# Moving the v products to the front, transposing a block of x by DMA, and four smaller re-orderings in a fused attention + MLP kernel

## Chip, cores and metric

One Trainium2 chip, one of its cores. The metric is device time in microseconds (us) of one execution; smaller is better. Each kernel was run several times. A profile is one of those executions, and its span is about 2 us shorter than the time of the same run, so spans are compared with spans and times with times.

Engines are called as the profile calls them: PE (TensorE, matmuls), DVE (VectorE), ACT (ScalarE), POOL (GpSimd), SP (SyncE, which here only issues DMAs; "SPq" in the listings).

## What the kernel must compute

```python
# x: 1 x 2048 x 1024, bf16; all weights bf16
xn  = layernorm(x)
qkv = xn @ wqkv                         # 1024 x 3072; 32 heads of 32
# each token attends to 8 tokens of its past, 2 apart:
logits = einsum(q, k[token - 2*w], w = 0..7) * 32**-0.5   # masked before token 0
s = (softmax(logits) @ v[token - 2*w]) @ wo
g = silu( (silu(xn @ w1) * (xn @ w3)) @ w2 )              # 1024 -> 3584 -> 1024
out = x + s * g
```

Of the kernel before, what the change touches and what calls it, by code (L numbers as in the profile page):

```python
# [8 lines left out]
FP32 = mybir.dt.float32  # L9
BF16 = mybir.dt.bfloat16  # L10
FP16 = mybir.dt.float16
ACTF = mybir.ActivationFunctionType
# [5 lines left out]
def kernel(  # L18
# [12 lines left out]
    P = 128  # L31
# [102 lines left out]
    def k4(name, shape=(2, CH), dt=FP32):  # L134
        return kk.tile([P, *shape], dt, tag="k4", name=name)
# [21 lines left out]
    def act_copy(out_, in_):  # L157
        with hp():
            nc.scalar.copy(out=out_, in_=in_)  # L159
# [3 lines left out]
    def flush():  # L163
        while pend:
            pend.pop(0)()
# [15 lines left out]
    def seven(key, A, B, e11, e12, e22, e21, snap=None):  # L181
        a11, a12, a22, s1, s2, s3, s4 = A
        b11, b21, b22, t1, t2, t3, t4 = B
        if snap is None:
            pa = bank2(f"a{key}")
            for i in I:
                mm(pa[:, i], a11[i], b11, True)
        pe = bank2(f"e{key}")
        for i in I:
            mm(pe[:, i], s1[i], t1, True)  # L190
        pb = bank2(f"b{key}")
        act_copy(pb[:], pa[:] if snap is None else snap)
        sp5 = k4(f"p{key}")
        act_copy(sp5[:], pe[:])
        if snap is None:
            for i in I:
                mm(pa[:, i], a12[i], b21, False)
            e11(pa)
        flush()
        for i in I:  # L200
            mm(pb[:, i], s2[i], t2, False)
        su2 = k4(f"u{key}")
        act_copy(su2[:], pb[:])
        for i in I:
            mm(pe[:, i], s4[i], b22, False)
        e12(pe, su2)
        run_hooks()
        for i in I:
            mm(pb[:, i], s3[i], t3, False)
        e22(pb, sp5)  # L210
        bg(pace["n"])

        def tail():
            for i in I:
                mm(pb[:, i], a22[i], t4, False)
            e21(pb)

        pend.append(tail)
# [74 lines left out]
    def xn_sums(b11, b21, b12, b22, o):  # L293
        nc.vector.tensor_sub(o[:, 0], b12, b11)
        nc.vector.tensor_sub(o[:, 1], b22, o[:, 0])
        nc.vector.tensor_sub(o[:, 2], b22, b12)
        nc.vector.tensor_sub(o[:, 3], b21, o[:, 1])
# [9 lines left out]



    def qkv_sums(w0, w1_, st):  # L310
        lo = lambda w: w.rearrange("p k (c two j) -> p k c two j", two=2, j=4)[:, :, :, 0]
        hi = lambda w: w.rearrange("p k (c two j) -> p k c two j", two=2, j=4)[:, :, :, 1]
        a11, a21, a12, a22 = lo(w0), hi(w0), lo(w1_), hi(w1_)
        s1, s2, s4 = [s.rearrange("p k (c j) -> p k c j", j=4) for s in st]
        s3 = hi(w0.bitcast(FP16))
        nc.vector.tensor_add(s1, a21, a22)
        nc.vector.tensor_sub(s2, s1, a11)
        nc.vector.tensor_sub(s4, a12, s2)
        nc.vector.tensor_sub(s3, a11, a21)
        pace["owed"] += 4.5  # L320

    def qkv_A(w0, w1_, st, g):
# [5 lines left out]
        sp = lambda q: [[sv[q][:, k, 2 * g + i, :] for k in range(KH)] for i in I]  # L328
        return pick(v0, 0), pick(v1, 0), pick(v1, 1), sp(0), sp(1), pick(v3, 1), sp(2)

    def park(t, c, j0, name):
        tl = k4(name, (2, CH), BF16)
        dst = (q_dram, k_dram, v_dram)[t][c, :, j0:j0 + 2, :]

        def fin():
            nc.sync.dma_start(out=dst, in_=tl[:])

        return tl[:], fin

    def qkv_dst(t, c, j0):  # L340
        if c == 0:
# [33 lines left out]
    def att_tile(shape, dt, name):  # L375
        return att.tile([P, *shape], dt, tag="a8", name=name)
# [26 lines left out]
    def scores(c, ws):  # L403
        q = qt[c]
        if c not in sc:
            sc[c] = att_tile((W, CH), BF16, f"Es{c}"), att_tile((NJ, CH), BF16, f"pt{c}")
        E, p_t = sc[c]
        for w in ws:
            o = HALO - DIL * w
            nc.vector.tensor_mul(p_t[:], q[:], kT[:, :, o:o + CH])  # L410
            yield 2.3
            nc.vector.tensor_add(p_t[:, 0:4, :], p_t[:, 0:4, :], p_t[:, 4:8, :])  # L412
            yield 1.25
            nc.vector.tensor_add(p_t[:, 0:2, :], p_t[:, 0:2, :], p_t[:, 2:4, :])
            yield 0.7
            nc.vector.tensor_add(E[:, w, :], p_t[:, 0, :], p_t[:, 1, :])
            yield 0.45
# [139 lines left out]

    tiles = {}

    free = [0, 1, 2, 3, 4, 6, 7, 8, 9]  # L560
    half = [0, 1]
    held = {}

# [57 lines left out]
    def mlp_up(b):  # L621
        work = [(g, fb) for fb in range(HB) for g in I] if b == 0 else []
        work += [(b, fb) for fb in range(HB, FB)]
        order = [fb for fb in range(b * HB, FB)]
        ahead = 2 + b
        for fb in order[:ahead]:
# [237 lines left out]
    def wo(b):  # L864
        (a11, a12, a21, a22, s1, s2, s3, s4), (b11, b12, b21, b22, t1, t2, t3, t4) = wx[b]
        if b == 1:
            xt4 = att_tile((2, 2, 2, CH), BF16, "xw")
            for u in I:
                for dh in I:
                    xw[u, dh] = xt4[:, u, dh]  # L870
                    nc.sync.dma_start(out=xw[u, dh], in_=out_rows(x_flat, 1, u, dh, 1))

        def product(ps, gp, lhs, rhs, first):
            for i in I:
# [43 lines left out]
    def out_rows(ap, b, u, dh, gp):  # L918
        g0 = ((2 * b + u) * NST + gp * 2) * P
        return ap[g0:g0 + 2 * P, dh * CH:(dh + 1) * CH].rearrange("(i p) n -> p i n", p=P)  # L920
# [48 lines left out]
    wq1 = qkv_load(0, 1, slot(6, (4, D)))  # L969
    for st in range(NST):  # L970
        (ln_act if st == 2 else ln_dve)(0, [st])
    qt[0] = att_tile((NJ, CH), BF16, "qt0")
    tps = [ln_tp(0, st, [], busy=(5, 0, 1, 1)[st]) for st in range(NST)]
    for a in I:
# [5 lines left out]
    wk1 = qkv_load(1, 1, rows(0, 4).rearrange("p (k n) -> p k n", k=4))  # L980
    sk = rows(4, 6, FP16).rearrange("p (q k n) -> p q k n", q=3, k=4)
    sk = [sk[:, q] for q in range(3)]
    b12 = k4("b12", (KH, CH), BF16)
    x_load(2)
    ln_dve(1, [0, 1])
    ln_dve(1, [2, 3])

    sq = rows(20, 6, FP16).rearrange("p (q k n) -> p q k n", q=3, k=4)
    sq = [sq[:, q] for q in range(3)]
# [1 line left out]
    Bq = B0, B_of(xT1[0], xT1[1], xT1[3], xs1)  # L991
    def tp1(*sts):
        for st in sts:
            ln_tp(1, st, [(b12[:].unsqueeze(1), slice(0, 1)), (xT[:, 2:3], slice(1, 2))])

    for t, (w0, w1_, ws) in enumerate(((wq0, wq1, sq), (wk0, wk1, sk))):
        first_two(f"f{t}", [qkv_A(w0, w1_, ws, g) for g in range(2)], B0[0], B0[1],
                  snap[2 * t:2 * t + 2], [qkv_copy(t, 0, 2 * g) for g in range(2)],
                  *((lambda: None, 4) if t == 0 else (lambda: tp1(2, 3), 0)))
        if t == 0:  # L1000
            tp1(0, 1)
    qkv_sums(wq0, wq1, sq)
    xn_sums(xT[:, 0], xT[:, 1], b12[:], xT[:, 2], xs)
    qkv_sums(wk0, wk1, sk)
    qkv_seven(0, 0, wq0, wq1, sq, None, snap[0:2])
    x_load(3)
# [4 lines left out]

    tr(2)

    wv = [slot(2 + 4 * h, (4, D)) for h in I]
    sva = slot(0, (2, 4, CH), FP16)
    sv = [sva[:, 0], sva[:, 1], rows(10, 2, FP16).rearrange("p (k n) -> p k n", k=4)]

    def before_v(g):
        if g == 0:
            for h in I:  # L1020
                qkv_load(2, h, wv[h])
            tr(3)
        else:
            with behind("v"):
                qkv_sums(*wv, sv)

# [5 lines left out]
                xn_sums(xT1[0], xT1[1], xT1[2], xT1[3], xs1)  # L1032
        w2_step()
    pace["n"] = PACE[0]
    qkv_seven(2, 0, *wv, sv, step0)
    pace["n"] = PACE[1]
    qkv_seven(1, 1, wk0, wk1, sk, step)
    flush()
    wq0 = qkv_load(0, 0, slot(8, (4, D)))
    wq1 = qkv_load(0, 1, rows(0, 4).rearrange("p (k n) -> p k n", k=4))  # L1040
    qkv_sums(wq0, wq1, sk)
    qkv_seven(2, 1, *wv, sv, step)
    qkv_seven(0, 1, wq0, wq1, sk, step)
    flush()
# [46 lines left out]
```

## The kernel before

Every large product is done block-wise with seven products in place of eight (sums of blocks are formed by DVE first, results recombined by DVE and ACT). Tokens come in four chunks of 512; `qkv_seven(t, b)`, built on `seven`, makes q (t = 0), k (1) or v (2) of the chunk pair b. Its first two products, a11·b11 and a12·b21, need neither sums nor the second chunk of the pair (called the second x block below), so `first_two` can do them early; it keeps a11·b11 as a snapshot for the later steps. The kernel before does that for q and k:

```python
for t, (w0, w1_, ws) in enumerate(((wq0, wq1, sq), (wk0, wk1, sk))):
    first_two(f"f{t}", [qkv_A(w0, w1_, ws, g) for g in range(2)], B0[0], B0[1],
              snap[2*t:2*t+2], ...)          # second x block: transposed by PE in between
    if t == 0:
        tp1(0, 1)
qkv_sums(wq0, wq1, sq)                       # DVE: sums of q's weight blocks
xn_sums(...)                                 # DVE: sums of x's blocks
qkv_seven(0, 0, ...); qkv_seven(1, 0, ...)   # q, k of pair 0
                                             # (v's weights load during the k products, into q's slots)
qkv_seven(2, 0, *wv, ...)                    # v of pair 0
qkv_seven(1, 1, ...)                         # k of pair 1
wq0, wq1 = qkv_load(...), qkv_load(...)      # q's weights once more (2 MB), and their sums
qkv_seven(2, 1, ...); qkv_seven(0, 1, ...)   # v, q of pair 1: the last projections before the MLP
```

Outputs that are not needed at once are parked: copied to a small ring of staging buffers (`k4`) and stored to DRAM by SP.

```python
def park(t, c, j0, name):
    tl = k4(name, (2, CH), BF16)             # the ring also serves the recombination copies
    ...
        nc.sync.dma_start(out=dst, in_=tl[:])
```

The same SP queue also carries the loads of x and of the weights and the DMA transposes of chunks 2 and 3, in order. `seven` releases held-back products (`flush`) early in its order:

```python
    flush()
    for i in I: mm(pb[:, i], s2[i], t2, False)
    su2 = k4(f"u{key}"); act_copy(su2[:], pb[:])
    for i in I: mm(pe[:, i], s4[i], b22, False)
```

Late in the kernel, four pieces of the residual x (`xw`, 256 KB each) load ahead of the `wo` weights.

## Time and profile before

| kernel before | |
|---|---|
| time, median (first 3 runs) | 732.58 us (732.14 to 734.04) |
| time in the later jobs (33 shared runs on three chips) | 731.8 to 735.7 us |
| span of the profiled run | 730.3 us, granted clock 0.998 |
| PE busy | 714.2 us (98%) |

Timeline (start, us, engine, line, operation, output<-inputs, and in brackets the idle time before it and what ended it):

```profile
148.98 1.23 DVE L351 TENSOR_TENSOR pk<-eq,uq 128x1024 bf16<-128x1024 f32 x1 [4.10 <-DMA q_dram<-pk]
167.04 0.69 DVE L603 TENSOR_TENSOR wring<-wring 128x1024 f16<-128x1024 bf16 x1 [1.95 <-DMA t_dram<-wring]
```

ACT's, for the exponential:

```profile
175.46 1.06 ACT L440 ACTIVATE Es<-Es 128x1024 f32<-128x1024 f32 x1 [2.53 <-DVE Es L438]
```

DVE waits for a parked q output to be stored, and 25 us later the exponential waits for DVE. The second line is a link between the two: DVE stands 1.95 us for a store by POOL of sums of w2 (t_dram, landed at 166.94 us), shortly before the operations that lead to the exponential. PE is not named in these lines.

### The profile page before, as it was taken

To read this page: it belongs to the slowest core of one execution; us is meant where nothing else is said; L and a number is where in the kernel's file an instruction comes from. 1 tells how busy PE (TensorE), PEld (TensorE's weight loads), DVE (VectorE), ACT (ScalarE), POOL (GpSimd) and SP (SyncE) were. 2 spreads that over 40 slices of the span, in tenths; PEclk is the share of its full clock that TensorE was granted. 3 is DMA by queue.
4 is the path that set the end of the run, shared out by engine and by line. 5 is a ranking of instruction groups with operands and counts; after the bars stand their busy time and mean duration, and the time that the engine had idled before them with its cause. 6 is when DMAs were issued, how large, how long until landed. Compare 5 with 4: busy or idle time off the path is not lost.

```text
span 730.3 us, 8739 instructions
## 1 busy us (share of the span) xinstructions
PE 714.2 (98%) x3312; PEld 345.8 (47%) x3367; DVE 624.2 (85%) x677; ACT 314.5 (43%) x328; POOL 99.3 (14%) x159
## 2 busy tenths in 40 slices
PE   7999999999999999999999999999999999999996
PEld 4655665654444444444444444444444444444442
DVE  7994688878798879878989899969859999979984
ACT  5744343437554546654545411123454555120233
POOL 0000000010400110142202010010345000510011
PEclk9999999999999999999999999999999999999999
DMA  9379148877756452467755745549799453666505
GB/s 321 140 177 286 57 147 281 254 210 262 200 204 231 143 175 87 141 194 242 231 174 191 240 156 186 178 162 375 188 283 326 136 159 102 192 190 203 179 5 111
DMA packets 117610, 140.82 MB, mean 193 GB/s; under 512 B 14273, under 2 KB 91073, under 8 KB 116929
## 3 DMA queue, kind: packets, MB, share of 16 engines
q1 hardware_dynamic: 103984, 101.47, 44.9%
q0 software_dynamic: 13584, 38.81, 17.2%
q8 instruction: 26, 0.43, 0.3%
q14 instruction: 16, 0.12, 0.1%
HBM read 98.30 MB, written 38.80 MB: 188 GB/s over the span
## 4 chain that ended last, share of the span: by engine, by line
PE 71%; DVE 18%; DMA 4%; issue 3%; ACT 3%; SPq 1%; POOL 0%; DVEq 0%; ACTq 0%; POOLq 0%
PE bm L149 17%; PE am L149 11%; PE em L149 11%; PE db L149 7%; PE bq L149 5%; PE de L149 4%; DVE pt L410 4%; PE eq L149 4%; PE da L149 3%; PE aq L149 3%; PE wb L149 2%; DVE pt L412 2%; PE we L149 2%; PE wa L149 2%; DMA q_dram<-pk 1%
## 5 line engine op out<-in xcount | busy, mean ns | idle before, releaser
L149 PEld LDWEIGHTS <-wring 128*128 128x128 f16 (+1 forms) x1920 | 201.7, 105 | 216.4 <-issue 5.2
L149 PEld LDWEIGHTS <-h_sb 128*128 128x128 f16 (+1 forms) x1088 | 114.0, 105 | 121.7 <-issue 1.0
L149 PE MATMUL bm<-xs,wring 128*128 128x512 f16 x504 | 117.3, 379 | 0.5 <-DVE h_sb L661 0.3
L149 PE MATMUL am<-xT,wring 128*128 128x512 bf16 x322 | 78.8, 379 | 0.9
L410 DVE TENSOR_TENSOR pt<-qt,kT 128x4096 bf16<-128x4096 bf16 x32 | 73.2, 2288 | 0.7
L149 PE MATMUL db<-wring,h_sb 128*128 128x512 f16 x336 | 73.2, 379 | 0.0
L465 DVE TENSOR_TENSOR BC<-Ep,vT 128x2048 bf16<-128x2048 bf16 x56 | 67.0, 1218 | 0.2
L646 DVE TENSOR_TENSOR um<-em,um 128x1024 f32<-128x1024 f32 x28 | 34.2, 1222 | 19.9 <-PE em L149 12.9
L648 ACT ACTIVATE g<-um 128x1024 bf16<-128x1024 f32 x28 | 29.6, 1057 | 49.7 <-DVE um L646 49.7
L149 PE MATMUL da<-wring,h_sb 128*128 128x512 bf16 x219 | 48.9, 379 | 0.3
L451 POOL DMA_DIRECT2D Ep<-pb x64 | 37.9, 600 | 25.5 <-DVE pb L447 18.5
L149 PE MATMUL bm<-h_sb,wring 128*128 128x512 f16 x168 | 39.7, 379 | 0.0
L149 PE MATMUL em<-xs,wring 128*128 128x512 f16 x168 | 39.7, 379 | 0.0
L412 DVE TENSOR_TENSOR pt<-pt 128x2048 bf16<-128x2048 bf16 x32 | 39.1, 1221 | 0.5
L475 DVE TENSOR_TENSOR oT<-oT,BC 128x2048 bf16<-128x2048 bf16 x32 | 39.1, 1220 | 0.5
L149 PE MATMUL em<-xT,wring 128*128 128x512 bf16 x161 | 39.2, 379 | 0.3
L159 ACT COPY bm<-am 128x1024 f32<-128x1024 f32 x28 | 28.0, 999 | 26.1 <-PE am L149 26.1
L159 ACT COPY pm<-em 128x1024 f32<-128x1024 f32 x28 | 28.4, 1013 | 19.3 <-PE em L149 19.2
L159 ACT COPY um<-bm 128x1024 f32<-128x1024 f32 x28 | 28.4, 1013 | 18.6 <-PE bm L149 18.2
L667 ACT CAST g<-bm 128x1024 bf16<-128x1024 f32 x28 | 28.3, 1010 | 17.6 <-PE bm L149 17.6
L351 DVE TENSOR_TENSOR pk<-eq,uq 128x1024 bf16<-128x1024 f32 x12 | 14.7, 1222 | 23.7 <-PE eq L149 13.2
L661 DVE TENSOR_TENSOR h_sb<-bm,pm 128x1024 bf16<-128x1024 f32 x21 | 25.6, 1218 | 5.3 <-PE bm L149 5.3
(176 smaller groups left out, 965.3 us busy)
## 6 DMA issues: line engine op xcount, KB each, us to landing
wring<-in_B_w_dram SPq DMA_DIRECT2D x61, 512.0 KB, 4.4
wring<-t_dram SPq DMA_DIRECT2D x16, 512.0 KB, 5.1
t_dram<-wring POOLq DMA_DIRECT2D x14, 512.0 KB, 4.5
wring<-in_A_wqkv_dram SPq DMA_DIRECT2D x6, 1024.0 KB, 8.0
wring<-t_dram SPq DMA_DIRECT2D x16, 384.0 KB, 5.5
wring<-in_B_w_dram SPq DMA_DIRECT2D x12, 384.0 KB, 4.7
wring<-in_A_x_dram SPq DMA_DIRECT2D x16, 256.0 KB, 6.1
Ep<-pb POOLq DMA_DIRECT2D x64, 64.0 KB, 4.9
```

Source lines behind the costliest of these rows:

```text
L149: anchor["pe"] = nc.tensor.matmul(ps, lhsT=lhs[k], rhs=rhs[k], start=(first and k == 0), stop=(k == n - 1), skip_group_check=not first,)
L159: nc.scalar.copy(out=out_, in_=in_)
L351: anchor["v"] = nc.vector.tensor_add(d, ps[:], a[0][:])
L410: nc.vector.tensor_mul(p_t[:], q[:], kT[:, :, o:o + CH])
L412: nc.vector.tensor_add(p_t[:, 0:4, :], p_t[:, 0:4, :], p_t[:, 4:8, :])
L451: nc.gpsimd.dma_start(out=pr[c][r:P:NR, :, sq * P:(sq + 1) * P], in_=pb[sq * 32:(sq + 1) * 32, :, :])
L465: nc.vector.tensor_mul(dst, E[:, w, :].unsqueeze(1).to_broadcast([P, n, CH]), vT[:, js, o:o + CH])
L475: nc.vector.tensor_add(A, A, B if w0 else C)
L646: v = nc.vector.tensor_add(su2[:], pe[:], su2[:])
L648: nc.scalar.activation(out=hl["g"][:, :, CH:], in_=su2[:], func=ACTF.Silu)
L661: anchor["v"] = nc.vector.tensor_add(h[:, :, CH:], pb[:], sp5[:])
L667: nc.scalar.copy(out=hl["g"][:, :, 0:CH], in_=pb[:])
```

## The change

The intent: do v's first products early as well, so that they cover the time in which DVE forms the sums of the second x block; take the transposes of that block from PE and give them to the DMA; keep v's weights resident so that q's need not be loaded twice; and move some stores, staging buffers, loads and one table load out of the way. The diff, cut to its core (cuts marked "# ..."):

```diff
@@ seven()
             e11(pa)
-        flush()
+            flush()
         for i in I:
             mm(pb[:, i], s2[i], t2, False)
         su2 = k4(f"u{key}")
         act_copy(su2[:], pb[:])
+        flush()                                   # held products one step later (groups with a snapshot)
@@ qkv_sums(..., again=False)
+        if again:                                 # q's sums the second time: 3 in place of 4
+            nc.vector.tensor_sub(s2, a22, s3)
+            nc.vector.tensor_add(s1, s2, a11)
+            nc.vector.tensor_sub(s4, a12, s2)
+            return
@@ park()
+    spare = [0, 1, 10, 11, 2, 3, 10, 11]
-        tl = k4(name, (2, CH), BF16)
+        tl = k4(name, (2, CH), BF16)[:] if t or c < 2 else rows(spare.pop(0), 1)...   # last q outputs
-            nc.sync.dma_start(out=dst, in_=tl[:])
+            (nc.gpsimd if c == 1 else nc.sync).dma_start(out=dst, in_=tl)
@@ mlp_up(b)
+        if b == 0:
+            nc.scalar.activation(out=scr[:], in_=rows(2, 1)[:, 0:1], func=ACTF.Silu)  # early table
@@ mlp_down(): late residual loads
-                    nc.sync.dma_start(out=xw[u, dh], ...)
+                    with behind("dl"):            # behind the wo weights
+                        nc.sync.dma_start(out=xw[u, dh], ...)
@@ start
+    wve = [att_tile((4, D), BF16, f"wve{h}") for h in I]
+    qkv_load(2, 0, wve[0][:])
+    for st in range(NST):
+        ln_dve(1, [st])
+        for a, d in ((0, b12), (1, xT[:, 2])):    # second x block, two half-size transposes a step
+            nc.sync.dma_start(out=d[...], in_=xt[1][...], transpose=True)
+        if st == 1:
+            qkv_load(2, 1, wve[1][:])
-    for t, (w0, w1_, ws) in enumerate(((wq0, wq1, sq), (wk0, wk1, sk))):
+    for t, (w0, w1_, ws) in enumerate(((wq0, wq1, sq), (wk0, wk1, sk), (wve[0][:], wve[1][:], sk))):
         first_two(...)
-        if t == 0:
-            tp1(0, 1)                             # PE transposes
-    wq0 = qkv_load(0, 0, slot(8, (4, D)))         # second load of q's weights
-    wq1 = qkv_load(0, 1, rows(0, 4)...)
-    qkv_sums(wq0, wq1, sk)
+    qkv_sums(wq0, wq1, sk, True)
 # ... (buffer places, the order of free slots, and anchors left out)
```

More of the change, by code (lines that the diff above doesn't have):

```diff
@@ L305, with qkv_sums @@
     B0 = B_of(xT[:, 0], xT[:, 1], xT[:, 2], xs)
-    def qkv_sums(w0, w1_, st):
+    def qkv_sums(w0, w1_, st, again=False):
         lo = lambda w: w.rearrange("p k (c two j) -> p k c two j", two=2, j=4)[:, :, :, 0]
@@ L315, in qkv_sums @@
         s3 = hi(w0.bitcast(FP16))
+        if again:
+            nc.vector.tensor_sub(s2, a22, s3)
+            nc.vector.tensor_add(s1, s2, a11)
+            nc.vector.tensor_sub(s4, a12, s2)
+            pace["owed"] += 3.4
+            return
         nc.vector.tensor_add(s1, a21, a22)
@@ L329, in qkv_A @@
         return pick(v0, 0), pick(v1, 0), pick(v1, 1), sp(0), sp(1), pick(v3, 1), sp(2)
+    spare = [0, 1, 10, 11, 2, 3, 10, 11]
     def park(t, c, j0, name):
-        tl = k4(name, (2, CH), BF16)
+        tl = k4(name, (2, CH), BF16)[:] if t or c < 2 else rows(spare.pop(0), 1).rearrange("p (j n) -> p j n", j=2)
         dst = (q_dram, k_dram, v_dram)[t][c, :, j0:j0 + 2, :]
         def fin():
-            nc.sync.dma_start(out=dst, in_=tl[:])
-        return tl[:], fin
+            (nc.gpsimd if c == 1 else nc.sync).dma_start(out=dst, in_=tl)
+        return tl, fin
     def qkv_dst(t, c, j0):
@@ L405, in scores @@
         if c not in sc:
-            sc[c] = att_tile((W, CH), BF16, f"Es{c}"), att_tile((NJ, CH), BF16, f"pt{c}")
+            sc[c] = att_tile((W, CH), BF16, f"Es{c}"), oT[:, 0] if c == 0 else att_tile((NJ, CH), BF16, f"pt{c}")
         E, p_t = sc[c]
@@ L558 @@
     tiles = {}
-    free = [0, 1, 2, 3, 4, 6, 7, 8, 9]
+    free = [8, 9, 0, 1, 4, 2, 3, 6, 7]
     half = [0, 1]
@@ L870, in wo @@
                     xw[u, dh] = xt4[:, u, dh]
-                    nc.sync.dma_start(out=xw[u, dh], in_=out_rows(x_flat, 1, u, dh, 1))
+                    with behind("dl"):
+                        nc.sync.dma_start(out=xw[u, dh], in_=out_rows(x_flat, 1, u, dh, 1))
         def product(ps, gp, lhs, rhs, first):
@@ L971 @@
         (ln_act if st == 2 else ln_dve)(0, [st])
+    wve = [att_tile((4, D), BF16, f"wve{h}") for h in I]
+    vsn = att_tile((2, 2, CH), FP32, "vsn")
     qt[0] = att_tile((NJ, CH), BF16, "qt0")
@@ L982 @@
     sk = [sk[:, q] for q in range(3)]
-    b12 = k4("b12", (KH, CH), BF16)
+    b12 = rows(12, 2).rearrange("p (k n) -> p k n", k=KH)
+    TPE = ()
+    qkv_load(2, 0, wve[0][:])
+    for st in range(NST):
+        ln_dve(1, [st])
+        if st not in TPE:
+            for a, d in ((0, b12), (1, xT[:, 2])):
+                nc.sync.dma_start(
+                    out=d[:, :, st * P:(st + 1) * P], in_=xt[1][:, st, a * CH:(a + 1) * CH], transpose=True,
+                )
+        if st == 1:
+            qkv_load(2, 1, wve[1][:])
     x_load(2)
-    ln_dve(1, [0, 1])
-    ln_dve(1, [2, 3])
     sq = rows(20, 6, FP16).rearrange("p (q k n) -> p q k n", q=3, k=4)
@@ L993, in tp1 @@
         for st in sts:
-            ln_tp(1, st, [(b12[:].unsqueeze(1), slice(0, 1)), (xT[:, 2:3], slice(1, 2))])
-    for t, (w0, w1_, ws) in enumerate(((wq0, wq1, sq), (wk0, wk1, sk))):
+            ln_tp(1, st, [(b12.unsqueeze(1), slice(0, 1)), (xT[:, 2:3], slice(1, 2))])
+    snap += [vsn[:, 0], vsn[:, 1]]
+    for t, (w0, w1_, ws) in enumerate(((wq0, wq1, sq), (wk0, wk1, sk), (wve[0][:], wve[1][:], sk))):
         first_two(f"f{t}", [qkv_A(w0, w1_, ws, g) for g in range(2)], B0[0], B0[1],
                   snap[2 * t:2 * t + 2], [qkv_copy(t, 0, 2 * g) for g in range(2)],
-                  *((lambda: None, 4) if t == 0 else (lambda: tp1(2, 3), 0)))
-        if t == 0:
-            tp1(0, 1)
+                  *((lambda: None, 4) if t == 0 else (lambda: None, 0)))
+    tp1(*TPE)
     qkv_sums(wq0, wq1, sq)
-    xn_sums(xT[:, 0], xT[:, 1], b12[:], xT[:, 2], xs)
+    xn_sums(xT[:, 0], xT[:, 1], b12, xT[:, 2], xs)
     qkv_sums(wk0, wk1, sk)
@@ L1012 @@
     tr(2)
-    wv = [slot(2 + 4 * h, (4, D)) for h in I]
+    wv = [wve[h][:] for h in I]
     sva = slot(0, (2, 4, CH), FP16)
@@ L1019, in before_v @@
         if g == 0:
-            for h in I:
-                qkv_load(2, h, wv[h])
             tr(3)
-        else:
             with behind("v"):
@@ L1034 @@
     pace["n"] = PACE[0]
-    qkv_seven(2, 0, *wv, sv, step0)
+    qkv_seven(2, 0, *wv, sv, step0, snap[4:6])
     pace["n"] = PACE[1]
@@ L1038 @@
     flush()
-    wq0 = qkv_load(0, 0, slot(8, (4, D)))
-    wq1 = qkv_load(0, 1, rows(0, 4).rearrange("p (k n) -> p k n", k=4))
-    qkv_sums(wq0, wq1, sk)
+    with behind("v"):
+        qkv_sums(wq0, wq1, sk, True)
     qkv_seven(2, 1, *wv, sv, step)
```

## The prediction

> **What bounds the kernel now.** I read the page's busy table first, then what TensorE (PE) waited for, then its timeline where the change works, and last the engines that those waits name.
>
> ```profile
> PE 714.2 (98%) x3312; PEld 345.8 (47%) x3367; DVE 624.2 (85%) x677; ACT 314.5 (43%) x328; POOL 99.3 (14%) x159
> ```
>
> PE is busy 714.2 of 730.3 us. Busy alone does not prove that the array streams, so I checked the pace: eight 128x512 matmuls follow each other in 1.73 us (107 pieces of the chain have just this length), 0.216 us each, from one end of the kernel to the other, and the granted clock is 1.00 until the tail. The kernel is bound by the number of matmuls; the other engines matter only where they make PE wait. Those waits are few:
>
> ```profile
> PE tp L280 <- DVE wring L254: 2.3, 1, 2.3
> PE warm L141 <- DVE warm L138: 1.3, 1, 1.3
> PE am L149 <- ACT bm L159: 0.7, 1, 0.7
> PE eq L149 <- DVE xs L294: 0.5, 1, 0.5
> PE zp L425 <- DVE dsu L823: 0.5, 1, 0.5
> PE bq L149 <- DVE pk L351: 0.3, 1, 0.3
> PE bm L149 <- DVE h_sb L661: 0.3, 1, 0.3
> ```
>
> The columns are total us, times, longest. The first two are the start (first load and layernorm), which the change leaves alone; the tail after the last matmul (about 724.3 to 730.3, output adds and stores) stays too. So 16.1 us of idle PE hold about 4 us of start and 6 us of tail, and everything the change can win back lies in small waits between 13 and 180 us, plus whatever PE work it deletes. That work is here, in PE's timeline (start, us, what, count):
>
> ```profile
> 13.25 7.07 PE L149 MATMUL af<-xT,wring 128*128 128x512 bf16 x32
> 20.15 1.06 PE L280 MATMUL tp<-ident,wring 128*128 128x128 bf16 x16
> 21.04 3.62 PE L149 MATMUL af<-xT,wring 128*128 128x512 bf16 x15
> 24.50 1.06 PE L280 MATMUL tp<-ident,wring 128*128 128x128 bf16 x16
> 25.40 3.62 PE L149 MATMUL af<-xT,h_sb 128*128 128x512 bf16 x16
> 29.57 2.35 PE L149 MATMUL eq<-xs,h_sb 128*128 128x512 f16 x10 [0.54 <-DVE xs L294]
> ```
>
> The two "tp" rows are the transposes of the second x block by matmul; what follows each starts 0.89 and 0.90 us after it. The last row is PE waiting for the first sum of that block.
>
> **What the Trainium skill says.** "DMA: Bandwidth & Descriptors", section "DMA Transpose (X-bar)", allows a transpose during a DMA for 2-byte types from the hardware queue only, with SBUF as the target: the new transposes meet that. The kernel before already has eight of them (128x1024 each), median 3.5 us from issue to landing, 1.3 to 3.3 us of SP's time each, so the trace agrees and prices them. The same page, section "Issuing engines are not separate DMA queues", says a second issuing engine only saves sequencer time, as all share 16 DMA engines; moving the parking stores to POOL should then relieve SP's order, not bandwidth. "SBUF — State Buffer", section "Who interferes with whom", warns that DMAs issued from GpSimd can be starved of descriptors by some VectorE modes; POOL's stores of before to s_dram, t_dram and h_dram land in 3.0 to 4.7 us (medians), SP's parking stores in 2.9 to 5.0, so this trace shows no such starvation. "ScalarE: Activation LUTs", section "What ACT_TABLE_LOAD costs", gives 1283 ns for the load; the trace has 1.28 us.
>
> **The change part by part.**
>
> Transposes: 32 matmuls of 128x128 leave PE, which issues 6672 rows instead of 6736 (weight loads counted). By the starts above that is 0.89 + 0.90 = 1.8 us of the bounding engine, the one certain gain. ACT loses eight PSUM copies of 0.6 us (4.8 us), gains two snapshot copies of 1.0 us. In their place SP issues eight half-size transposes.
>
> Early v products: the same 32 matmuls (32 x 0.216 = 6.9 us) move ahead of the q products, none is added. By PE's order they now stand where DVE's sums of block two were late. DVE reached that first sum at 28.29 us; its queue ahead of it changes by about one 1.2 us sum more and one 0.65 us statistic less. PE will need it at 13.25 + 3 x 6.9 = 33.95 us instead of about 28.9. The 0.7 us wait (0.92 us between starts less one matmul) goes.
>
> The v weights: before, they could only load into slots of q, behind parking stores and transposes on SP:
>
> ```profile
> 54.13 0.34 SPq L336 DMA_DIRECT2D k_dram<-pk  x1
> 54.52 3.32 SPq L291 DMA_TRANSPOSE h_sb<-wring  x1
> 57.93 0.77 SPq L336 DMA_DIRECT2D k_dram<-pk  x1
> 58.75 5.74 SPq L291 DMA_TRANSPOSE h_sb<-wring  x3
> ```
>
> ```profile
> 62.13 1.23 DVE L351 TENSOR_TENSOR pk<-eq,uq 128x1024 bf16<-128x1024 f32 x1 [6.35 <-DMA k_dram<-pk]
> 63.93 1.23 DVE L351 TENSOR_TENSOR pk<-bq,pq 128x1024 bf16<-128x1024 f32 x1 [0.58 <-DMA k_dram<-pk]
> ```
>
> A store waits in SP's order, its buffer is not freed, DVE stands 6.35 us, and PE's next group slips: bq starts at 65.21 where 62.98 + 8 x 0.216 = 64.71 was due (0.50), and the next loses 0.28. With the first v products done, the v weights long landed and these stores on POOL, I expect 0.8 us back. The reload of q's weights (two 1 MB loads) and one of its four sums (1.2 us of DVE) also go; no PE wait in the trace hangs on them. The q outputs parked in other rows free staging buffers; ACT waited 2.18 us and DVE 4.1 us once each for such stores, but PE was not held, so: 0.
>
> Held product one step later: it only applies to the first six q, k, v groups. It gives the copies another 1.7 us to finish. The gaps left there, at 38.6 and 47.3 us, are 0.3 and 0.17 us; with a 0.28 us gap near 117 I count 0.5 us for this and the shifted phases.
>
> Silu table early: before, three table loads stand in one MLP step:
>
> ```profile
> 167.87 1.28 ACT L642 ACT_TABLE_LOAD   x1
> 171.64 1.28 ACT L440 ACT_TABLE_LOAD   x1
> 176.53 1.28 ACT L648 ACT_TABLE_LOAD   x1
> ```
>
> PE lost about 1.3 us at 177 to 180 (0.30 and 0.65 as idle, the rest as slips). The built order has the first load moved before the MLP; the other two stay, ten loads in all as before. The Exp between them waits 2.53 us for DVE anyway, so only part comes back: 0.6 us.
>
> Late residual loads: four 256 KB loads that were issued from 652.46 us move behind the wo loads (after 687 us). They are first used at about 722 us, and PE shows no wait for weights at 650 to 690 us: 0.
>
> New costs. PSUM has four double banks. The third pair of first products needs the banks that the first pair leaves, and in ACT's new order those copies stand behind a k copy that needs the second pair finished at 25.3 us: 25.3 + 1.0 + 1.0 = 27.3 us against PE's 27.05 us, so with hand-over some 0.4 to 0.5 us. Second, SP's order puts the second half of the v weights behind the first four transposes. Loads are at their limit then (about 1 MB in 2.7 us: landings at 18.08 and 20.79), so the first v half should land near 23.5 and the second near 28 to 29; PE wants them at 27.05 and 30.5. The last transposes should land at 30 to 32, sums wanting them by about 32. That is tight; I charge 0.5 us (three chances in ten of some 1.5 us).
>
> Sum: -1.8 - 0.7 - 0.8 - 0.5 - 0.6 + 0.5 + 0.5 = -3.4 us. 732.6 - 3.4 = 729.2 us.
>
> **The rivals.** (1) The load phase becomes the bound: 8 MB of loads and eight slow transposes before 32 us, one SP queue in order; a transpose that took 3.3 us of issue while 1 MB loads were in flight speaks for it, the later need (33.95) against. PE would stand 3 to 5 us at 27 to 36, and the time would be 731 to 734. (2) The removed waits are hidden or replaced: DVE, 85% busy over all and full from 10 to 50 us, becomes the next to be late; then only the transposes count and the time is 730.5 to 731. Its single-step layernorm adds only some small operations, and it loses a sum, so I give this a quarter. (3) Everything works and DVE's lighter queue also removes the waits at 177 and 487 us (0.6): 727. (4) POOL's stores land late behind its own descriptor work and hold staging buffers at 36 to 86 us, as SP's did: about 1 us back, 730.
>
> **Range and chances.** 2% is 14.7 us. Faster by that is out of reach: 1.8 us of PE work and about 5 us of waits are all there is. Slower by that needs a stall of 18 us in a start that lasts 35. The runs before spread 732.1 to 734.0. Range 726.5 to 731.9; faster 0.01, same 0.975, slower 0.015.
>
> **What would show it.** Right: no 128x128 matmuls after 13 us; the v products at about 27 to 34 us; no wait of eq on the xs sum; DVE's 6.35 us wait gone and PE without a gap at 51 to 70; by 90 us PE some 3 us ahead of before, and about 0.5 more by 180; from there to the end the same pace and the same tail. Wrong: gaps of over 1 us in PE at 27 to 36 us ended by a weight load, a transpose or ACT's copies; parking stores on POOL that end DVE or ACT waits; a lead that shrinks after 180 us.

## The result

The changed kernel takes 726.87 us (median of 5 runs, 726.07 to 727.05), the kernel before in the same rounds 733.87 us (732.14 to 734.07): ratio 0.9908, 95% interval 0.9894 to 0.9923. Ratios here and below are the mean time of one kernel's runs over the mean of the other's in the same rounds, so not quite the ratio of the quoted medians. That is 7 us or 0.9% faster: within 2%, as expected, and about twice the 3.4 us that the prediction summed up. The median lies 0.4 us above the lower end of the range that the prediction gave (726.5 us), and two of the five runs lie below it.

The page of the changed kernel, busy line:

```profile
PE 715.2 (99%) x3335; PEld 344.1 (47%) x3335; DVE 622.8 (86%) x678; ACT 313.9 (43%) x325; POOL 111.7 (15%) x171
```

and, from what PE waited for (total us, times, longest):

```profile
PE warm L141 <- DVE warm L138: 1.3, 1, 1.3
PE de L149 <- ACT dsp L159: 1.1, 1, 1.1
PE af L149 <- DMA wve<-in_A_wqkv_dram: 0.4, 1, 0.4
```

Of the waits that the prediction lists after the start-up ones, all five are gone (am, eq, zp, bq, bm); three new ones have come: for the second half of v's weights, for a copy of dsp near 675 us, and 0.2 us at 16 us for q's weights. PE's busy time is 1 us longer although it does 1.8 us less: the records of some matmuls are missing from either trace (3312 and 3335 counted), so busy sums of PE are no measure of 1 us here. What does measure it is when each kernel reaches the same matmul. For the second pair of profiles (the repeats below) the lead of the changed kernel is 0.6 us at the first transposes (the first loads landed earlier in that run, which is chance), 4.1 us at 84 us, 4.5 at 172 and 5.3 at 179, 5.9 at 482, 6.2 from 580 to 674 and 6.0 at the end.

PE's timeline where the early v products stand:

```profile
26.50 3.62 PE L149 MATMUL af<-xT,wve 128*128 128x512 bf16 x16
30.54 3.67 PE L149 MATMUL af<-xT,wve 128*128 128x512 bf16 x16 [0.42 <-DMA wve<-in_A_wqkv_dram]
34.05 1.89 PE L149 MATMUL eq<-xs,h_sb 128*128 128x512 f16 x8
```

The products run from 26.5 to 34 us, and the xs sum that PE used to wait for is ready when it is wanted. The transposes behind it are as late as was feared: SP issued the eight from 15.25 to 30.52 us, the last landed at 32.29, DVE stood 3.97 us for one, and the sum was done at 33.2, 0.85 us before PE wanted it. Their landings show what they were late behind: the first landed at 24.59 us, 0.5 us after the first half of v's weights (24.10), and the last four at 30.91, 31.39, 31.87 and 32.29, right after the second half (30.49).

### The profile page after: what moved, and what is told of

Read it like the earlier page. It is cut to its first block, busy times and chain, and to the rows that moved or that the text cites. A ratio compares the mean times of both kernels' runs of the same rounds, so it can differ in the third digit from the quotient of the medians. Undisturbed runs are those within 1.5% of the kernel's fastest.

```text
span 725.4 us, 8725 instructions
## 1 busy us (share of the span) xinstructions
PE 715.2 (99%) x3335; PEld 344.1 (47%) x3335; DVE 622.8 (86%) x678; ACT 313.9 (43%) x325; POOL 111.7 (15%) x171
## 4 chain that ended last, share of the span: by engine, by line
PE 92%; DVE 3%; ACT 2%; DMA 1%; issue 1%; SPq 0%; DVEq 0%; ACTq 0%
PE bm L149 20%; PE am L149 13%; PE em L149 13%; PE db L149 10%; PE bq L149 9%; PE de L149 7%; PE da L149 7%; PE eq L149 5%; PE aq L149 3%; PE wb L149 2%; PE we L149 2%; PE wa L149 2%; DVE stats L250 1%; DMA wve<-in_A_wqkv_dram 1%; PE af L149 1%
## 5 line engine op out<-in xcount | busy, mean ns | idle before, releaser
L149 PEld LDWEIGHTS <-wring 128*128 128x128 f16 (+1 forms) x1824 | 187.9, 103 | 207.5 <-issue 1.9
L149 PEld LDWEIGHTS <-h_sb 128*128 128x128 f16 (+1 forms) x1056 | 109.6, 104 | 119.4 <-issue 2.0
L419 DVE TENSOR_TENSOR pt<-qt,kT 128x4096 bf16<-128x4096 bf16 x24 | 55.0, 2290 | 0.7
L421 DVE TENSOR_TENSOR pt<-pt 128x2048 bf16<-128x2048 bf16 x24 | 29.3, 1222 | 0.4
L962 POOL DMA_DIRECT2D out_dram<-h_sb x12 | 15.1, 1512 | 94.7 <-DVE h_sb L961 94.6
```

The lines of the kernel that those rows point to most:

```text
L149: anchor["pe"] = nc.tensor.matmul(ps, lhsT=lhs[k], rhs=rhs[k], start=(first and k == 0), stop=(k == n - 1), skip_group_check=not first,)
L419: nc.vector.tensor_mul(p_t[:], q[:], kT[:, :, o:o + CH])
L421: nc.vector.tensor_add(p_t[:, 0:4, :], p_t[:, 0:4, :], p_t[:, 4:8, :])
L962: nc.gpsimd.dma_start(out=rows_, in_=g, accum_op=ALU.add)
```

## The experiments

Twelve kernels in three jobs, each job on a chip of its own with its own runs of the kernel before. Where two kernels stood in different jobs they are compared through their ratios to before; the changed kernel itself ran in the first job (ratio 0.9898) and before that (0.9908), so 0.990 stands for it below, and 0.001 is 0.73 us. Three parts were not undone on their own and have no share below: q's weights no longer loaded twice, the changed order of free slots, and the changed buffer places.

| run | what | median us | ratio to before, 95% interval |
|---|---|---|---|
| b_again | before, unchanged | 733.59 | 1.0002 (0.9985 to 1.0019) |
| a_again | changed kernel, unchanged | 726.13 | 0.9898 (0.9885 to 0.9911) |
| a_pe_transpose | transposes back on PE | 728.73 | 0.9931 (0.9918 to 0.9944) |
| a_late_v | no early v products | 734.52 | 1.0017 (1.0004 to 1.0029) |
| a_park_k4 | last q outputs in the ring again | 728.77 | 0.9947 (0.9928 to 0.9966) |
| a_no_silu | no early Silu table | 726.38 | 0.9915 (0.9900 to 0.9930) |
| a_park_sp | parking stores all on SP again | 726.99 | 0.9920 (0.9904 to 0.9936) |
| a_best | the two new waits attacked | 725.70 | 0.9908 (0.9893 to 0.9924) |
| b_park_oT | before, last q outputs elsewhere | 730.97 | 0.9968 (0.9956 to 0.9980) |
| b_silu | before, with a Silu preload | 739.10 | 1.0067 (1.0031 to 1.0104) |
| a_flush_old | held products early again | 726.90 | 0.9915 (0.9902 to 0.9928) |
| a_xw_early | residual loads early again | 730.88 | 0.9971 (0.9955 to 0.9987) |

All results were correct.

### The two kernels again (b_again, a_again)

No edit.

> The kernel before, unchanged, for a second trace and for the spread. The measured change (-6.7 us) is twice the predicted one, while the two profiled spans differ by only 4.9 us. Theory A (the run profiled before was a lucky one): the ratio to itself is 1.000 within 0.002, and this trace is up to 2 us longer than the first, with the excess in one or two places that can be named. Theory B (the profiles are typical and the clock outside them differs): the trace is again within 0.4 us of 730.3 and the places of the waits are the same.

> The changed kernel, unchanged, beside the others on this chip: ratio 0.991 within 0.002. In its trace the second half of the v weights again holds PE for 0.4 to 0.7 us near 30 us (second half landing near 30.5), and the gap of 1.2 to 1.3 us near 675 us (PE de waits for ACT dsp) is there again if it comes from the order of VectorE's work, absent if it was chance.

Measured: 733.59 and 726.13 us, spans 729.6 and 723.6 us. The result repeats. Neither theory holds as it was put: the second trace of before is 0.7 us shorter than the first, not longer and not within 0.4 us; the places of the waits are the same, as theory B had it. Past the first transposes PE's gaps of before are in both of its profiles to within 0.2 us, except one: near 65 us it lost 0.50 us the first time and 0.08 us the second. The wait for v's weights in the changed kernel came once (0.42 us) and not the second time; the one for dsp was 1.1 us and then 0.2 us. The spans differ less than the times because of which runs were profiled: both of before were shorter than its medians (732.26 and 731.56 us), the first one of the changed kernel was the longest of its five (727.05 us).

### Transposes by PE in the changed kernel (a_pe_transpose)

```diff
-    TPE = ()
+    TPE = (0, 1, 2, 3)
     # and tp1(0, 1) after the q products, tp1(2, 3) within the k products, as before
```

> The change with the transposes of the second x block back on PE (32 matmuls of 128x128, eight ACT copies), the rest kept. Theory A (the transposes are worth their PE time and no more): PE gains 1.8 us of work, but SP's queue is free, the second v half lands by 27 us and the 0.6 us gap near 30 us goes: about +1.2 us against the changed kernel, ratio near 0.9925. Theory B (DMA transposes choke the start): the time is equal to the changed kernel or below it. Theory C (eight ACT copies more make the first pair's banks late): +2.5 us or more, with PE gaps ended by ACT at 20 to 32 us.

Measured: 728.73 us, 2.6 us above a_again on the same chip (2.4 us by the ratios). The trace shows the 1.8 us of PE work and a wait for ACT to copy the transposed block out of PSUM:

```profile
PE af L149 <- ACT xT L287: 0.7, 1, 0.7
```

So in the changed kernel these transposes on PE cost more than their matmuls: 1.8 us of work, 0.7 us of waiting for the copies. The kernel before has no such wait: there the products start 0.89 and 0.90 us after each row of transposes (the prediction's lines). Theory A's size was nearly met, theory C's gap was there, and theory B is out.

### No early v products (a_late_v)

```diff
-    ... enumerate(((wq0, wq1, sq), (wk0, wk1, sk), (wve[0][:], wve[1][:], sk))):
+    ... enumerate(((wq0, wq1, sq), (wk0, wk1, sk))):
-    qkv_seven(2, 0, *wv, sv, step0, snap[4:6])
+    qkv_seven(2, 0, *wv, sv, step0)
```

> The change without the early v products: v's first 32 matmuls stand again inside the v groups, the DMA transposes stay. Theory A (the early v products are the cover for the transposes' landing): PE reaches the first sum product near 27 us while the transposes land near 32 us, so a gap of 5 to 6 us opens at 27 to 33 us; no later place can give it back, and the 0.6 us wait for the v weights goes: +4.5 to +5.5 us against the changed kernel, ratio near 0.998. Theory B (the order of products does not matter, other buffers decide): within 0.7 us of the changed kernel.

Measured: 734.52 us, 8.4 us slower than a_again and slightly slower than before. PE's timeline:

```profile
33.91 3.60 PE L149 MATMUL eq<-xs,h_sb 128*128 128x512 f16 x8 [6.97 <-DVE xs L295]
37.30 2.20 PE L149 MATMUL bq<-xs,h_sb 128*128 128x512 f16 x8
```

PE stands 7 us for the sum that hangs on the slow transposes. It is more than expected because of the second half of the cost: the eight matmuls of the first row take 3.6 us, nearly all at 0.43 us, before the pace returns to 0.216, which adds about 2 us. The Trainium skill, "TensorE: Matmul & The Clock Gate", section "What's actually happening", says that PE falls to half clock after an idle window of about 3.4 us and needs about as long a busy time to return; the trace agrees (6.97 us idle, then 0.427 us from start to start for nine matmuls). Two parts of the change thus hang together: the DMA transposes alone would have lost time, and the early v products are what hides them.

### The last q outputs in the ring again (a_park_k4)

```diff
-    tl = k4(name, (2, CH), BF16)[:] if t or c < 2 else rows(spare.pop(0), 1)...
+    tl = k4(name, (2, CH), BF16)[:]
```

> The changed kernel with the last q outputs staged in the common ring of buffers again, as before. Theory D: VectorE waits some 2 to 4 us for q_dram stores near 145 to 150 us, the Exp comes late and PE's 1.2 us at 173 to 180 come back: 1.0 to 1.5 us slower than the changed kernel, 727.1 to 727.7. Rival (the prediction's count for this part, zero): VectorE waits or not, PE does not, 726 to 726.5.

Measured: 728.77 us, ratio 0.9947 against 0.990: about 3 us slower, with a spread of 727.5 to 731.7 us. The size is above what theory D gave, and the place is another. The gaps are not at 173 to 180 us but earlier. PE's timeline, then DVE's:

```profile
143.41 1.89 PE L149 MATMUL bq<-h_sb,wring 128*128 128x512 f16 x8 [0.83 <-ACT uq L159]
160.65 1.67 PE L149 MATMUL bq<-h_sb,wring 128*128 128x512 f16 x7 [1.05 <-DVE pk L360]
```

```profile
157.47 1.23 DVE L360 TENSOR_TENSOR pk<-eq,uq 128x1024 bf16<-128x1024 f32 x1 [5.20 <-DMA q_dram<-pk]
```

DVE stands 5.2 us for the store of an earlier q output, since all of the ring is on its way to DRAM; ACT waits for DMA stores in the same stretch. Against a_again 2.2 us are lost in the trace, all of it at these two places.

### The kernel before with only that part (b_park_oT)

The opposite test. The rows that the change uses are not free in the kernel before, so the outputs go to oT, which nothing uses until then; PE's order is the same.

```diff
-    tl = k4(name, (2, CH), BF16)
+    tl = k4(name, (2, CH), BF16)[:] if t or c < 2 else oT[:, c - 2, j0:j0 + 2]
```

> The kernel before with one thing changed: its last eight q outputs are staged in oT, which is unused until then, in place of the common ring of buffers; PE's order is the same. Theory D (the stores of the ring hold VectorE and ScalarE, and the Exp of that step comes late): VectorE's 4.1 us wait for a q_dram store near 149 us and the 2 us wait near 167 us go, PE's gaps at 177 to 180 us (1.3 us in all) go, the runs spread less, and the time falls by 1.3 to 2.5 us (ratio 0.9966 to 0.998). Rival (the prediction: PE was not held by these stores, zero): ratio 0.999 to 1.001, gaps at 177 to 180 us stay.

Measured: 730.97 us, ratio 0.9968: 2.3 us faster than before, in runs that spread by 1.2 us. Theory D holds. DVE's timeline, at the operation that stood 4.10 us for q_dram in before, and ACT's:

```profile
147.87 1.23 DVE L351 TENSOR_TENSOR oT<-eq,uq 128x1024 bf16<-128x1024 f32 x1 [2.34 <-PE eq L149]
```

```profile
168.52 1.28 ACT L642 ACT_TABLE_LOAD   x1
172.26 1.28 ACT L440 ACT_TABLE_LOAD   x1
174.07 1.06 ACT L440 ACTIVATE Es<-Es 128x1024 f32<-128x1024 f32 x1 [0.52 <-DVE Es L438]
175.14 1.28 ACT L648 ACT_TABLE_LOAD   x1
```

DVE now waits for PE, the healthy direction; POOL's t_dram store leaves at 157.72 us in place of 158.48 and lands at 165.40 in place of 166.94, so DVE's wait for it is gone as well; the exponential waits 0.52 us in place of 2.53; and PE has no gap at 177 to 180 us any more (0.5 and 0.8 us beyond the pace in before). All three table loads are still in this step. These gaps are 1.3 of the 2.3 us; where the rest was won no trace shows. In this profile the gain is hidden by a longer stall at 65 us (1.47 us), which is the next point.

### The Silu table (a_no_silu, b_silu)

```diff
 # a_no_silu: the changed kernel
-        if b == 0:
-            nc.scalar.activation(out=scr[:], in_=rows(2, 1)[:, 0:1], func=ACTF.Silu)
 # b_silu: the kernel before
+        if b == 0:
+            nc.scalar.activation(out=scr[:], in_=eps_t[:], func=ACTF.Silu)
```

> The changed kernel without the early Silu table load. Theory D (VectorE is free of its store waits, so the Exp reaches ScalarE 6 us earlier, and that alone removes the idle of PE at 177 to 180 us): within 0.3 us of the changed kernel, 726 to 726.5, PE without a gap over 0.3 us at 168 to 180. Rival S (the table load in the middle of the MLP step was the cost, as the prediction had it at 0.6): 0.6 to 1.2 us slower, 726.8 to 727.4, with PE gaps after bm and am near 170 to 176 us again.

Measured for a_no_silu: 726.38 us, ratio 0.9915, not told apart from the changed kernel by its interval, and in the trace there is nothing at all: ACT's timeline

```profile
163.71 1.28 ACT L651 ACT_TABLE_LOAD   x1
167.50 1.28 ACT L449 ACT_TABLE_LOAD   x1
169.26 1.06 ACT L449 ACTIVATE Es<-Es 128x1024 f32<-128x1024 f32 x1 [0.47 <-DVE Es L447]
```

has the table load back in the step, the exponential is not later, and PE has no gap there. With b_park_oT this is shown from both sides: the tables cost PE nothing; DVE's wait for the stores did.

> The kernel before with the early Silu table load added, nothing else. Prediction: 0.6 us faster (ratio 0.9992), gaps at 177 to 180 us halved. Theory D (the Exp waits for VectorE, not for the table): the gaps stay within 0.3 us, ratio 0.9995 to 1.0005. Its trace also serves as another look at where the kernel before varies from run to run up to 165 us.

Measured for b_silu: 739.1 us, 731.6 to 742.4 us. As a test of the table it failed: the constant it reads is ready at once, so the built order put the load at 2.33 us, far too early to help, and the gaps at 187 and 189 us stayed. The built order of the first 30 us also shifted on several engines, so it is not "before plus one thing". But it showed where the kernel before varies. SP's DMA transposes at 55 to 73 us (count, shortest/median/longest in ns; in before the longest is 3320):

```profile
L291 SPq DMA_TRANSPOSE h_sb<-wring x3: 1383/2126/12956, 55.3 to 59.6; - x3
```

One transpose held SP for 13 us, from 59.56 us on, and DVE, then PE, stood in the same stretch (DVE's timeline, then PE's, of b_silu):

```profile
72.97 1.22 DVE L351 TENSOR_TENSOR pk<-bq,pq 128x1024 bf16<-128x1024 f32 x1 [8.96 <-DMA k_dram<-pk]
```

```profile
74.25 1.87 PE L149 MATMUL bq<-xs,h_sb 128*128 128x512 f16 x4 [8.56 <-DVE pk L351]
```

This is the 65 us stall that before has too, at 0.08 to 0.5 us in its two profiles, 1.47 us in b_park_oT and 8.6 us here. It does not begin with that transpose: the k store that ended DVE's 8.96 us had left SP earlier, at 57.54 us, and landed at 72.85, 0.6 us after a 1 MB load by which POOL fetches q of the next chunk (issued at 55.51, landed at 72.22). POOL's timeline of before has the same load:

```profile
53.52 0.72 POOL L395 DMA_DIRECT2D qt<-q_dram  x1 [51.06 <-DMA q_dram<-pk]
```

It landed at 61.83 us; the first k store, issued at 54.13 and so ahead of the transpose at 54.52, landed at 62.01; DVE went on at 62.13. In b_again these three are 61.19, 61.36 and 61.48 us, in b_park_oT 62.40, 62.57 and 62.70. Before's two 1 MB loads of v's weights were in flight as well (issued at 49.4 and 49.9, landed at 56.0 and 58.7). SP's order adds to it: the second k store left at 57.93, behind a transpose of 3.3 us. So the chain is bulk loads in flight, store, DVE, PE, with a length that varies. In the changed kernel v's weights load at the start and this load of q goes out at 133 us, and no profile of it or of its variants has the stall. No run takes these loads away alone, so their part is read from the traces, not isolated.

### Parking stores on SP again (a_park_sp)

```diff
-            (nc.gpsimd if c == 1 else nc.sync).dma_start(out=dst, in_=tl)
+            nc.sync.dma_start(out=dst, in_=tl)
```

> The changed kernel with all parking stores on SP again, early v products kept. If moving those stores to POOL is what cured VectorE's 6.35 us wait for k_dram stores (the transposes hold SP in order): that wait of several us returns near 50 to 65 us and PE loses 0.5 to 1.0 us there, 726.7 to 727.3. Rival (the early v products have taken the work whose sums were late, so the stores' place doesn't matter): 726 to 726.5, PE without gaps at 55 to 70 us.

Measured: 726.99 us, 725.6 to 728.0, ratio 0.9920. DVE's wait for a k_dram store came back at 1.23 us (67 us), not several, and PE shows no gap at 55 to 70 us. By the ratio up to 1.5 us may be lost in a typical run, but the intervals overlap, and the profiled run's span is only 0.3 us above a_again's. With the stores back on SP the stall of before does not return, so moving them to POOL is not what removed it; the bulk loads have left this stretch here too (see the Silu table above). Whether POOL's part is worth anything stays open.

### Held products early again (a_flush_old)

```diff
             e11(pa)
-            flush()
+        flush()
 ...
         act_copy(su2[:], pb[:])
-        flush()
```

> The changed kernel with the held products issued one step earlier again, as before. Prediction's term for this: 0.5 us slower than the changed kernel, with gaps of 0.2 to 0.3 us back near 36 and 45 us. Rival: with the early v products VectorE and ScalarE are ahead, the copies are done in time either way: within 0.2 us, 726 to 726.5.

Measured: 726.90 us, ratio 0.9915 (0.0015 above 0.990, with overlapping intervals). The trace says where it would come from: a gap at 43 us, and a smaller one at 52 us (0.18 us beyond the pace). PE's timeline:

```profile
43.59 1.89 PE L149 MATMUL bq<-xs,wring 128*128 128x512 f16 x8 [0.63 <-DVE pk L359]
```

0.8 us at this place and 0.2 us at the next, 1.0 us in the trace; in before the same two places lose 0.30 and 0.17 us. The prediction's 0.5 us has the right sign and order; the times alone would not show it.

### Residual loads early again (a_xw_early)

```diff
-                    with behind("dl"):
-                        nc.sync.dma_start(out=xw[u, dh], ...)
+                    nc.sync.dma_start(out=xw[u, dh], ...)
```

The built order of all engines but SP is that of the changed kernel.

> The changed kernel with the late residual loads issued early again, ahead of the wo weights, as before. Prediction: no PE wait hangs on them, 0: 726 to 726.5. Rival: they fill the queue just where PE's gap at 675 us and VectorE's 6 us wait for vT at 654 us stand; then these two waits change and the time moves by 0.3 to 1 us, either way.

Measured: 730.88 us, ratio 0.9971: 5 us slower, more than either expectation. DVE's timeline at 656 us and PE's at 678 us:

```profile
656.43 1.23 DVE L474 TENSOR_TENSOR oT<-Ep,vT 128x2048 bf16<-128x2048 bf16 x1 [8.33 <-DMA vT<-v_dram]
```

```profile
678.73 7.89 PE L149 MATMUL de<-wring,h_sb 128*128 128x512 bf16 x28 [3.38 <-ACT dsp L159]
```

and the same two places in the changed kernel:

```profile
654.66 1.22 DVE L474 TENSOR_TENSOR oT<-Ep,vT 128x2048 bf16<-128x2048 bf16 x1 [6.03 <-DMA vT<-v_dram]
```

```profile
676.96 3.40 PE L149 MATMUL de<-wring,h_sb 128*128 128x512 bf16 x15 [1.09 <-ACT dsp L159]
```

From DVE's operation to PE's restart it is 22.3 us in both (678.73 - 656.43 and 676.96 - 654.66) and in a_again: in these kernels a fixed chain of DVE work, so PE's time there is set by when vT has landed. With the 1 MB of residuals in flight it is 7.9 us from the issue of the vT load to DVE's start on it, without them 4.7 and 5.6 us. In the first case PE stands 3.4 us and then runs seven matmuls at half pace (0.43 us): 4.9 us in all against a_again.

Why did the same early loads cost nothing in the kernel before? There vT was used at

```profile
658.30 1.23 DVE L465 TENSOR_TENSOR oT<-Ep,vT 128x2048 bf16<-128x2048 bf16 x1 [4.65 <-DMA vT<-v_dram]
```

and the copy of dsp that PE waits for came here (DVE has one more operation ahead of it than in the changed kernel):

```profile
680.57 0.99 ACT L159 COPY dsp<-de 128x1024 f32<-128x1024 f32 x1
```

It ended at 681.56 us, and PE, which had started this row of products at 675.70, came to it 28 matmuls later, at 681.75, without a gap: 0.2 us to spare, and 0.3 us in b_again. The changed kernel brings PE there 6 us sooner, but the vT load is issued only 1.6 us sooner. POOL's copy ahead of that load shows why (before, then changed kernel):

```profile
649.13 1.17 POOL L387 COPY vT<-vT 128x64 bf16<-128x64 bf16 x1 [16.27 <-DVE BC L465]
```

```profile
644.15 4.57 POOL L396 COPY vT<-vT 128x64 bf16<-128x64 bf16 x1 [30.50 <-DVE BC L474]
```

The copy takes 4.57 us in place of 1.17, ending when a row of DVE operations ends. The Trainium skill, "SBUF — State Buffer", section "Who interferes with whom", says that a DVE instruction with two inputs in SBUF contends with a GpSimd instruction that reads SBUF, and that who issues first wins. The long copy fits this: it ends 0.09 us after the fourth of that row. The page alone does not explain the short one, which ended 0.09 us after one DVE operation though the next had begun. The copy takes 4.57 or 4.58 us in all ten profiles of the changed kernel and its variants and 1.17 us in all four of before and its variants; no run isolates the reason. What is shown is the rest: without the later residual loads, the changed kernel would have given back about 5 of its 7 us at 675 us.

### A version to beat both (a_best)

```diff
+    qkv_load(2, 1, wve[1][:])          # ahead of the transposes, not after half of them
 ...                                    # and in mlp_down(): both dsp copies ahead of the two Silus on ACT
+                anchor["c22"] = nc.scalar.copy(out=sp5[:], in_=pe[gp][:])
+            if gp == 1:
+                with hp(), behind("c22"):
+                    for k in G2: silu(g_tile(b, 1, 1, k), held22[k][:])
```

> Two small waits that the changed kernel's traces showed are attacked: 0.42 us at 30 us for the second half of the v weights (its load now goes out ahead of the transposes) and 1.1 us at about 675 us for a copy of dsp (both copies of that row now stand ahead of the two Silus in ScalarE's order). If both waits are real costs of the typical run: 0.5 to 1.5 us faster than the changed kernel, 724.7 to 725.7 (ratio to before about 0.988). Rival: the waits only move to VectorE's sums of block two or to the next step (VectorE is 86% busy): 726 to 726.5, no difference.

Measured: 725.70 us, ratio 0.9908. Both waits are gone from its trace, and the time cannot be told from that of the changed kernel: the waits were about 0.4 and 0.2 to 1.1 us in single runs, so they are worth less in the mean than these rounds resolve. A miss as an improvement.

## Why the prediction was right, and where its sum was off

**Class right, mechanism right in outline.** Nothing near 2% could move, and the time fell through deleted PE work and deleted small waits, as reasoned. The class was the safe part. The number was not: the sum came out at half, rival 3 (727 us) is nearer than the prediction's own 729.2, and the range held by 0.4 us. The signs named for "right" appeared: no 128x128 matmuls past the start, no wait of eq on the xs sum, DVE's 6.35 us wait gone. The lead was to be some 3 us by 90 us, and 0.5 more by 180; it was 3.5 us (4.1 less the chance 0.6 at the start) and 1.2 more, and it then grew further, to 6.2 us, where the same pace was expected.

**Transposes, -1.8 us.** Right for before, whose trace shows 0.89 and 0.90 us and no wait for the copies. Undone in the changed kernel they cost 2.4 us, but 0.7 us of that is a wait for ACT's copies that before does not have.

**Early v and the xs wait, -0.7 us.** Right: the wait is gone. a_late_v shows that this step is also the cover without which the DMA transposes would cost over 8 us; rival 1 was that near.

**v weights and parking stores, -0.8 us.** Gone in both profiles, but the cause was misread in part. "A store waits in SP's order" does not fit the 6.35 us wait: its store left at 54.13 us, ahead of the transposes, and landed at 62.01, right behind POOL's 1 MB load of q, while the loads of v's weights were in flight too. Moving the stores to POOL was not needed for the cure (a_park_sp). The term is a varying one, 0.1 to 1.5 us in three profiles of kernels with before's start and 8.6 in one; before's longer typical runs (about 2 us over its own two profiled runs) fit this, but no profile of the unmodified kernel caught a long one, so that stays likely and not shown.

**Parked q outputs, 0.** This step of the prediction failed most. "PE was not held" was read from the gap that directly follows DVE's wait; PE paid 25 us later, where the delayed exponential held the MLP step at 177 to 180 us. Undone it costs about 3 us, done alone in before it gains 2.3 us.

**Silu table, -0.6 us.** Measured 0. The gaps were put down to the table loads that stood nearest; they belonged to the step above. So part of the right gap was counted for the wrong reason. The two terms together were -0.6 and are about -2.3 us.

**Held products, -0.5 us.** About right: the gaps of 0.30 and 0.17 us are gone, and undone in the changed kernel it costs 1.0 us in one trace, within the noise of the times. The 0.28 us gap near 117 us that was counted with them is still there, at 113 us.

**Late residual loads, 0.** As a gain over before this may still be near 0 (PE had 0.2 to 0.3 us to spare there), but as a part of the change it is worth 5 us: it keeps the gain of the others. The prediction asked whether PE waits for these loads in before; it did not ask what they collide with once PE comes 6 us sooner. A lead "that shrinks after 180 us" was named as a sign of being wrong; this is the place where it would have, and where it did by 1.3 us in the first profile and 0.4 us in the second, with the late loads in place.

**New costs, +0.5 and +0.5 us.** The wait for PSUM banks did not appear. The v weights cost 0.42 us in one profile and 0 in the other.

**The wait at 487 us** (0.6 us, zp on dsu), given only to rival 3, went as well: there DVE now waits 0.80 us for PE. Which part of the change brought that about was not tested.

Summed as measured (transposes, xs wait, v weights and stores at the mean of before's two profiles, q outputs, held products by the gaps of before, the wait at 487 us; then the two larger new waits at the mean of two profiles): -1.8 - 0.7 - 0.6 - 2.3 - 0.5 - 0.6 + 0.2 + 0.6 = -5.7 us, against 7 measured. The terms come from different runs and lean on each other, so this is a check of size only. The 1.3 us left over stand in no trace; before's typical runs lie about 2 us above its profiled ones and a_again's only 0.8 us above its own, which is of that size. Against the -3.4 of the prediction the largest single difference is the q outputs.

## What to carry to other kernels

Before an order of issue is blamed for a late transfer, compare when the transfer left and when it landed, and look for what else was in flight. An idle time of an engine that is not the bound can be paid for by the bounding engine one or two steps later, so follow a delayed operation to its last consumer before counting it as zero. When a change brings the bounding engine forward by several microseconds, list the transfers late in the kernel whose issue does not move forward with it: their slack shrinks by the whole lead, and bulk loads that were free next to them are free no more. And a transfer or transpose that is slow but early is only cheap as long as other work covers it; take out one part at a time to see which parts hold each other up.

## What the Trainium skill lacked or had wrong

- "DMA: Bandwidth & Descriptors", section "Issuing engines are not separate DMA queues", calls the sequencer's time to start a DMA usually small relative to the DMA itself. For DMA transposes on SP it is not: 1.2 to 5.0 us each here, and 12.96 us once while a 1 MB load issued earlier had not landed, against 0.3 to 0.5 us for most plain 256 KB stores beside them.
- The same page, section "DMA Transpose (X-bar)", says nothing of how this time scales on this chip. Half-size transposes (128x512) held SP for 1.2 us or more, as full ones (128x1024) did: the shortest were 1.20 and 1.23 us. So halving them saved SP nothing per transpose.
- "Advanced Engine Details and Errata", section "X-Bar Transpose (TRN2)", puts DMA transposes level with ordinary DMAs. At the start of the changed kernel they were somewhat slower: once the load ahead had landed, the last four of 128 KB landed 0.42 to 0.48 us apart, the 256 KB loads of x behind them 0.64 and 0.73 us apart. That is about 285 against 380 GB/s, an estimate from these times. No run measures transposes without other traffic.
